# Convolution taps in PSUM banks, the norm's multiply on GpSimd, and output sums in tiles of their own: a convolution and SwiGLU layer on one core

## The chip, the cores and the metric

The kernel runs on one core of a Trainium2 chip, as one launch. The metric is the device time in microseconds (us), the median of several runs. A core has TensorE (PE, matrix products, with its weight loads shown as PEld), VectorE (DVE), ScalarE (ACT) and GpSimd (POOL); SyncE (SP) issues the DMA transfers. SBUF is the working memory, PSUM the eight banks of 128 x 512 fp32 that TensorE writes.

## The reference

```python
def _attn_ref(x, weight):              # x (8, 4096, 192), weight (8 heads, 7 taps)
    w = np.exp(weight - np.max(weight, axis=-1, keepdims=True))
    w = w / (np.sum(w, axis=-1, keepdims=True) + 1e-09)
    x_pad = np.concatenate([np.zeros((B, K - 1, D)), x], axis=1)
    idx = np.arange(S)[:, None] + np.arange(K)[None, :]
    x_unf = x_pad[:, idx, :].reshape(B, S, K, H, D // H)
    return np.einsum('hk,bskhg->bshg', w, x_unf).reshape(B, S, D)

def _moe_ref(x, w_gate, w_val, w_out, rms_g):   # x (32768, 192), d_ff 1536
    rms = np.sqrt(np.mean(x * x, axis=-1, keepdims=True) + 1e-06)
    xn = x / rms * rms_g
    g = xn @ w_gate
    silu = g * (1.0 / (1.0 + np.exp(-g)))
    val = xn @ w_val
    return (silu * val @ w_out).astype(np.float32)
```

A causal convolution of seven taps, whose weights each head has of its own, feeds a layer with an RMS norm, two projections from 192 to 1536, silu(g) * val, and a projection back to 192. All is in fp32.

## The kernel before

**Tiling.** The 32768 tokens are cut into 32 "pairs", each two tiles of T = 512 tokens (g = 0 and 1). The 1536 hidden features are twelve chunks of 128; three chunks and both token tiles make a "unit", four units to a pair. The value h = silu(g) * val of a unit lies in a tile `ht` of six slices of 128 x 512, v = 0 to 2 for g = 0 and 3 to 5 for g = 1.

**The product stage** of a pair. Both projections are done with 15 products a unit where 18 would be plain: sums of the inputs (`XSUM`, line 67, made by `x_sum` into `xc`, eleven a pair) and of the weights go in, and the results are combined afterwards. TensorE's rows are used in halves: the half LOW makes gate results (h = 0), UPP value results (h = 1). A matmul of 64 x 512 is one step; a pair has 4 x 15 x 2 = 120 such steps (`product`, line 693, recorded at L699). Each half has four PSUM banks, taken from and given back to the lists `free`.

`Unit.do` (line 705) holds the small operations between the banks. Their names in the order are engine (A, V, G, D for ScalarE, VectorE, GpSimd, DMA), action, half or step, and unit:

- S40, S50, S41, ...: copy a bank to a temporary tile of 128 x 512 (L660 on ScalarE, L664 on VectorE). F0, F2, F3: copy one bank to another.
- D5: add a temporary to a bank (L715). C: the sum "c" of the temporaries 40 and 50 (L719). R0 to R5: a bank plus or minus a temporary (L725), into a temporary for the gate and into `ht` for the value.
- G: silu on ScalarE (L738). M: multiply silu by value into `ht` (L745); M4 reads the value from a bank, the others from `ht`.

The temporaries come from the list `tiles`, first in, first out: 5 single ones, 6 in two `tls` tiles, and 3 in the tile `nt`, 14 in all.

**The output stage** of a pair. The projection back is again made with fewer products: seven "forms" of six steps k where eight would be plain, 126 steps in all (`OUTS`, line 764, `products`, line 803, recorded at L817). The left sides are h itself and four sums of h (`sum`, line 838, recorded at L845, 24 a pair on GpSimd): form 1 of `sum` overwrites a21, form 2 a11, form 4 a12, and form 3 goes to the tile `early`. Three banks (X, Y, Z) collect the results; VectorE adds them (L863) and transposes blocks into `o_sb` (L833), which is stored.

**Work for later pairs**, in the same streams: x of pair p + 3 is loaded (`load`); pair p + 2 gets its convolution, seven operations "cv" of 128 x 1536 (`tap`, L413 on ScalarE for the first, L417 on VectorE for the rest), the squares "sq" on ScalarE (L429), their reduction "red" on VectorE (L440 to L442), the power -1/2 "pow" on GpSimd (L446, L449), the spreading of the factors "bc" (two copies at L454 and a transpose at L458) and the multiply "mul" (L465), all on VectorE; the result goes to DRAM ("place") and comes back transposed as `xb` of pair p + 1 ("fetch", L613), from which the x sums "X" are made (L622).

**The order** of all this is written out by hand, in `ORDER` (line 90), one list for every pair: "p2" is two TensorE steps, "VR1.0.0" result 1 of half 0 of unit 0 on VectorE; a name that ends in "-" acts for the pair before. Every engine runs its own instructions in this order and waits by semaphores for what it needs. Pair 0 has a start of its own (`START`, `LATER`, `plain`, `outer`).

Of the kernel before, what the change touches and what calls it, by code (L numbers as in the profile page):

```python
# [11 lines left out]
F32 = mybir.dt.float32  # L12
# [7 lines left out]
def kernel(  # L20
# [67 lines left out]

    SPAN = 1509
    ORDER = (  # L90
        "p2 Dplace- VT12- p2 AS40.0.0 AS40.1.0 p2 VF0.0.0 AF0.1.0 p2 VT22- AS50.1.0 Dst0-",
        "VS50.0.0 p2 AS41.0.0 VS41.1.0 Acv0 GC.0.0 p2 VS00.1.0 Dst1- p2 GC.1.0 VD5.1.0",
        "AS00.0.0 p2 VD5.0.0 AS42.1.0 AS42.0.0 p2 AS51.0.0 VR1.0.0 AS51.1.0 p2 VR1.1.0",
        "AG1.0.0 VR0.0.0 p2 AF2.0.0 VR0.1.0 AF2.1.0 p1 AF3.0.0 VF3.1.0 p2 AS44.0.0 p1",
        "AS44.1.0 VR5.0.0 p2 VR2.0.0 AG5.0.0 p1 VR2.1.0 AG2.0.0 p2 VR3.1.0 AG4.0.0 GM2.1.0 p1",
        "VR5.1.0 p1 AS40.0.1 VR3.0.0 p1 AS40.1.1 p1 VM4.1.0 AF0.0.1 p1 AG3.0.0 p1 VF0.1.1",
        "AS50.0.1 p1 Vcv1 p1 AS50.1.1 GC.0.1 p1 AS41.0.1 p1 AS41.1.1 p1 GC.1.1 AS00.0.1 p1",
        "AS00.1.1 VD5.0.1 p2 GM5.1.0 VD5.1.1 AS42.0.1 p1 AS42.1.1 p1 VR1.0.1 AS51.1.1 p1",
        "GM1.1.0 AS51.0.1 p1 VR1.1.1 p1 VR0.0.1 p1 AF2.0.1 VR0.1.1 p1 AF2.1.1 p1 Vcv2 AF3.0.1",
        "p1 AF3.1.1 p1 AS44.0.1 p1 AS44.1.1 p1 VR5.0.1 AG1.0.1 p1 VR2.1.1 p1 AG0.0.0 p1",  # L100
        "VR2.0.1 GM0.1.0 p1 AG4.0.1 VR3.1.1 p2 VM4.1.1 AS40.0.2 GM3.1.0 p1 VR3.0.1 AS40.1.2",
        "p1 AG5.0.1 VR5.1.1 p1 GM1.1.1 AF0.0.2 p1 VS50.0.2 AF0.1.2 p2 AS50.1.2 GS3.0 VS41.0.2",
        "p1 AG2.0.1 p1 AS41.1.2 VS00.0.2 p1 GS3.1 AG0.0.1 p1 VC.1.2 AS00.1.2 p2 GS1.0 VD5.1.2",
        "AS42.0.2 p1 AS42.1.2 VD5.0.2 p1 GC.0.2 VR1.0.2 p1 AS51.0.2 p1 AS51.1.2 VR1.1.2 p1",
        "GM2.1.1 VR0.0.2 p1 AF2.0.2 p1 VR0.1.2 AF2.1.2 p1 AG3.0.1 p1 AF3.0.2 p1 GM3.1.1",
        "VS44.0.2 AF3.1.2 p1 AS44.1.2 p1 VR2.0.2 AG1.0.2 p2 VR2.1.2 AG0.0.2 p1 VR5.0.2",
        "AG2.0.2 GM0.1.2 p1 VR5.1.2 AG4.0.2 p2 VR3.1.2 AS40.0.3 GM5.1.1 p1 AG5.0.2 VR3.0.2 p1",
        "AS40.1.3 VM4.1.2 p1 GM1.1.2 AF0.0.3 p1 VS50.0.3 AF0.1.3 p2 VM0.1.1 AS50.1.3 GS1.1 p1",
        "AS41.0.3 VS41.1.3 p1 AS00.0.3 p1 VM5.1.2 GS3.2 AG3.0.2 p1 VD5.0.3 AS00.1.3 p2",
        "VD5.1.3 AS42.0.3 GS1.2 p1 AS42.1.3 VS51.0.3 p1 AS51.1.3 VR1.0.3 p1 GM2.1.2 p2",  # L110
        "VR0.1.3 p1 GC.0.3 AF2.0.3 p1 VR1.1.3 AF2.1.3 p1 VR0.0.3 GM3.1.2 p1 VF3.1.3 p1",
        "AF3.0.3 p1 AS44.0.3 VC.1.3 GS3.4 p1 AS44.1.3 VR2.0.3 p1 AG1.0.3 p1 VR5.0.3 AG0.0.3",
        "GS3.3 p1 VR5.1.3 AG4.0.3 VR3.0.3 p2 AG5.0.3 GS1.3 p1 VM0.1.3 p1 AG2.0.3 p1 VM1.1.3",
        "p2 AG3.0.3 p1 GS2.1 Dfetch VR2.1.3 p3 Vcv3 p2 GS2.0 p6 Ac1 VM4.1.3 p3 Vcv4 p1 GS3.5",
        "p6 GS2.3 p2 VM5.1.3 p3 VR3.1.3 p1 GS1.5 p2 As7 p1 VX3 p2 GS2.2 p1 VM3.1.3 p3 VM2.1.3",
        "p2 GS1.4 Vcv5 p6 GS2.4 p3 VX0 p3 GS2.5 Vcv6 p6 GS4.5 p2 VX1 p1 Asq p2 VX2 GS4.0 p3",
        "VT11 p1 Ac2 p1 Dload p1 GS4.2 Vred p6 GS4.4 p4 VX4 p1 Gpow p1 VX7 p3 VX8 p3 VX9 p3",
        "VX6 p1 GS4.1 p4 VC22 p2 VX5 GS4.3 p3 Vbc p3 Vmul p12 VC21 p2 VX10 p3 VT21",
    )

    cst = ctx.enter_context(tc.tile_pool(name="cst", bufs=1))
# [100 lines left out]
    kept = [early[:, i].rearrange("p (j d) -> p j d", d=D) for i in range(3)]  # L222
    kept = itertools.cycle(kept)
    flat3 = early[:].rearrange("p i n -> p (i n)")
    diff = [flat3[:, k * T : (k + 1) * T] for k in range(FC // 2)]
    nw = 4 * (FC // 2) * (D // 2)
    tw = x0[:].rearrange("p j d -> p (j d)")[:, 0:nw].rearrange(
        "p (i k d) -> p i k d", i=4, k=FC // 2
# [178 lines left out]
    def tap(p, k, eng="V"):  # L407
# [12 lines left out]
        if k == K - 1:  # L420
            x_sb.pop(p)

    yn, st = {}, {}
    nb = TB // Q

# [18 lines left out]
    def factor(p):  # L444
# [2 lines left out]
            out=r, in0=r, scalar1=1.0 / D, scalar2=1e-6, op0=ALU.mult, op1=ALU.add  # L447
        )
        nc.gpsimd.tensor_tensor(out=r, in0=r, in1=nhalf[:, 0 : nb * NR], op=ALU.pow)  # L449

    def spread(p):
        ss, t, r = st[p]
        for c in range(nb):
            nc.vector.tensor_copy(  # L454
                out=by_head(t)[:, c],
                in_=r[:, c, :].rearrange("p (b o) -> p b o", o=1).to_broadcast([P, NR, H]),
            )
        nc.vector.transpose(out=ss[:], in_=t[:])  # L458

    def scale(p):  # L460
        ss = st.pop(p)[0]
        y = y_of(p)
        ys.pop(p)
        yn[p] = yn[p][:].rearrange("p (a t) -> p a t", t=TB)
        nc.vector.tensor_tensor(  # L465
            out=yn[p].rearrange("p a t -> p t a"), in0=y,
            in1=ss[:].rearrange("p (t o) -> p t o", o=1).to_broadcast([P, TB, GS]), op=ALU.mult,
        )
# [177 lines left out]
    def put(at, do):  # L646
        heapq.heappush(line, (at, next(tick), do))
# [25 lines left out]
    class Unit:  # L673
# [31 lines left out]
        def do(self, eng, act, h):  # L705
# [9 lines left out]
                nc.vector.tensor_tensor(out=b, in0=b, in1=t[:], op=ALU.add)  # L715
                tiles.append(t)
            elif kind == "C":
                c, t = tl.pop(("40", h)), tl.pop(("50", h))
                engine[eng].tensor_tensor(out=c[:], in0=c[:], in1=t[:], op=ALU.add)  # L719
                tl["c", h] = c  # L720
                tiles.append(t)
            elif kind == "R":
                k, s = RESULT[v]
                t = tl.pop((k, h))
# [31 lines left out]
    def out_sums():  # L756
# [5 lines left out]
                yield  # L762

    OUTS = (
        (1, "X", 0, 6), (7, "Z", 0, 6), (2, "Y", 0, 6), (6, "X", 0, 6), (4, "Z", 0, 3),
        (5, "X", 0, 6), (4, "Z", 3, 6), (3, "X", 0, 6),
    )
    HOME = {"X": 0, "Y": 1, "Z": 1}
    RIGHT = {1: B11, 2: B21, 3: B22, 4: T4, 5: T1, 6: T2, 7: T3}

    class Pair:
# [9 lines left out]
        def left(self, form, k):  # L781
            if form == 7:
                return diff[k]
            g, f = {1: (0, 0), 6: (0, 0), 2: (0, 1), 3: (0, 1), 5: (1, 0), 4: (1, 1)}[form]
            return self.h(g, 2 * k + f)

        def bank(self, b):
# [50 lines left out]
        def sum(self, form, k, eng):  # L838
            a11, a12 = self.h(0, 2 * k), self.h(0, 2 * k + 1)
            a21, a22 = self.h(1, 2 * k), self.h(1, 2 * k + 1)  # L840
            dst, a, b, op = {
                1: (a21, a21, a22, ALU.add), 2: (a11, a21, a11, ALU.subtract),
                3: (diff[k], a11, a21, ALU.subtract), 4: (a12, a12, a11, ALU.subtract),
            }[form]
            engine[eng].tensor_tensor(out=dst, in0=a, in1=b, op=op)  # L845

# [36 lines left out]
        def ahead(self, eng, act):  # L883
# [4 lines left out]
            elif act == "load":  # L888
                load(p + 3)
            elif p + 2 < PAIRS:  # L890
                if act[0:2] == "cv":
                    tap(p + 2, int(act[2:]), eng)
                else:
                    {
                        "sq": square, "red": reduce, "pow": factor, "bc": spread, "mul": scale,
                        "place": lambda p: done(place(p)),
                    }[act](p + 2)
# [185 lines left out]
    base = NU * SPAN  # L1083
    put(base - 1, lambda: outer(0, hts, base))
    put(base + 450, functools.partial(fetch, 1))
    put(base + 1317, lambda: tiles.extend(t[:, i, :] for t in tl6 for i in range(3)))
    put(base + 3000, lambda: tiles.extend(flat[:, i * T : (i + 1) * T] for i in range(3)))
    c = base + 200

    def later(it, *places):  # L1090
# [58 lines left out]
```

## Time and profile before

| | before |
|---|---|
| time, median of 3 runs | 3021.5 us (3017.94 to 3021.96) |
| span of the profiled run | 3016.8 us |
| VectorE busy | 2802.2 us (93%) |
| TensorE busy | 2741.1 us (91%) |
| GpSimd busy | 2226.0 us (74%) |
| ScalarE busy | 1648.5 us (55%) |
| chain that ended last: PE, DVE, issue | 55%, 32%, 8% of the span |
| DVE taps of 1536 (L417), 186 | 427.0 us |
| DVE multiply of the norm (L465), 31 | 90.1 us |
| GpSimd sums of h (L845), 744 | 996.0 + 290.6 us |

Busy times are summed over the whole span and are averages over stages that differ. The chain of waits is followed back from the last instruction to what released each; its shares say which engine the end waited for. A row of a group gives the line of the kernel, engine, operation, outputs and inputs with shapes, the count, then busy time in us and the mean of one in ns, then the idle time before it and what ended that.

### The profile page before, as it was taken

To read this page: it belongs to the slowest core of one execution; us is meant where nothing else is said; L and a number is where in the kernel's file an instruction comes from. 1 tells how busy PE (TensorE), PEld (TensorE's weight loads), DVE (VectorE), ACT (ScalarE), POOL (GpSimd) and SP (SyncE) were. 2 spreads that over 40 slices of the span, in tenths; PEclk is the share of its full clock that TensorE was granted. 3 is DMA by queue.
4 is the path that set the end of the run, shared out by engine and by line. 5 is a ranking of instruction groups with operands and counts; after the bars stand their busy time and mean duration, and the time that the engine had idled before them with its cause. 6 is when DMAs were issued, how large, how long until landed. Compare 5 with 4: busy or idle time off the path is not lost.

```text
span 3016.8 us, 91662 instructions
## 1 busy us (share of the span) xinstructions
PE 2741.1 (91%) x39418; PEld 1883.3 (62%) x39418; DVE 2802.2 (93%) x3655; ACT 1648.5 (55%) x3061; POOL 2226.0 (74%) x1513
## 2 busy tenths in 40 slices
PE   6999988999889998889988899988999889999999
PEld 3665666655666566666666665666666666666666
DVE  8899999999999999999999999999999999999986
ACT  5366544566445664446654466544566445665455
POOL 4886678866778767787667886677866778766777
PEclk9999999999999999999999999999999999999999
DMA  5412122121222112221222212122111222122110
GB/s 125 76 26 51 34 56 55 31 47 34 55 56 34 43 34 55 55 39 38 48 41 56 44 40 49 34 55 55 34 43 34 55 55 35 43 42 47 44 34 13
DMA packets 445208, 139.33 MB, mean 46 GB/s; under 512 B 385024, under 2 KB 419328, under 8 KB 444673
## 3 DMA queue, kind: packets, MB, share of 16 engines
q1 hardware_dynamic: 444240, 133.44, 22.3%
q8 instruction: 308, 5.05, 0.7%
q14 instruction: 100, 0.82, 0.1%
q10 hardware_dynamic: 560, 0.03, 0.0%
HBM read 83.87 MB, written 49.55 MB: 44 GB/s over the span
## 4 chain that ended last, share of the span: by engine, by line
PE 55%; DVE 32%; issue 8%; POOL 2%; DMA 1%; ACT 1%; SPq 1%; DVEq 0%; ACTq 0%; POOLq 0%
PE ps L699 52%; DVE xc L622 9%; DVE ht L745 8%; DVE y L417 6%; PE ps L817 2%; DVE o_sb L833 2%; DVE s L440 2%; DVE s L454 1%; DVE ht L725 1%; POOL ht L845 1%; PE ps L913 1%; POOL wf L346 1%; ACT tls L738 1%; DVE nt L863 0%; DVE tile L863 0%
## 5 line engine op out<-in xcount | busy, mean ns | idle before, releaser
L699 PE MATMUL ps<-xc,wf 64*128 64x512 f32 x4960 | 1344.8, 600 | 33.0 <-DVE o_sb L833 19.5
L699 PEld LDWEIGHTS ps<-xc,wf 64*128 64x128 f32 x4960 | 665.5, 187 | 555.9 <-issue 331.7
L845 POOL TENSOR_TENSOR ht<-ht 128x512 f32<-128x512 f32 x558 | 996.0, 1806 | 9.7
L699 PE MATMUL ps<-xb,wf 64*128 64x512 f32 x2480 | 751.3, 595 | 0.0
L817 PE MATMUL ps<-ht,wo_sb 128*32 128x128 f32 x13392 | 419.5, 280 | 69.5 <-DVE nt L863 27.1
L660 ACT ACTIVATE tile<-ps 128x512 f32<-128x512 f32 (+1 forms) x508 | 297.1, 599 | 330.4 <-PE ps L699 316.3
L699 PEld LDWEIGHTS ps<-xb,wf 64*128 64x128 f32 x2480 | 340.3, 188 | 216.1 <-issue 181.0
L660 ACT ACTIVATE tls<-ps 128x512 f32<-128x512 f32 x678 | 389.1, 602 | 123.3 <-PE ps L817 69.8
L817 PEld LDWEIGHTS ps<-ht,wo_sb 128*32 128x32 f32 x13392 | 381.4, 113 | 118.1 <-POOL r L449 46.9
L660 ACT ACTIVATE ps<-ps 128x512 f32<-128x512 f32 (+1 forms) x651 | 349.2, 579 | 190.7 <-PE ps L817 87.6
L817 PE MATMUL ps<-ht,x 128*32 128x128 f32 x13392 | 392.3, 274 | 54.1 <-POOL ht L845 37.8
L417 DVE SCALAR_TENSOR_TENSOR y<-xh,tp,y 128x1536 f32<-128x1536 f32 x186 | 427.0, 2296 | 0.2
L817 PEld LDWEIGHTS ps<-ht,x 128*32 128x32 f32 x13392 | 365.9, 110 | 75.4 <-POOL ht L845 51.7
L745 POOL TENSOR_TENSOR ht<-ht,tile 128x512 f32<-128x512 f32 x195 | 251.2, 1299 | 214.3 <-ACT tile L738 214.3
L660 ACT ACTIVATE nt<-ps 128x512 f32<-128x512 f32 (+1 forms) x302 | 175.0, 594 | 304.1 <-PE ps L817 157.3
L745 POOL TENSOR_TENSOR ht<-ht,tls 128x512 f32<-128x512 f32 x145 | 194.0, 1338 | 147.5 <-ACT tls L738 147.5
L845 POOL TENSOR_TENSOR early<-ht 128x512 f32<-128x512 f32 x186 | 290.6, 1578 | 0.0
L817 PE MATMUL ps<-early,x 128*32 128x128 f32 x4464 | 154.0, 287 | 84.7 <-issue 56.0
L719 POOL TENSOR_TENSOR tile<-tile,tls 128x512 f32<-128x512 f32 x51 | 86.9, 1711 | 180.4 <-DVE tls L664 134.5
L429 ACT ACTIVATE yn<-y 128x1536 f32<-128x1536 f32 x31 | 46.0, 1485 | 296.5 <-DVE y L417 296.5
L817 PEld LDWEIGHTS ps<-early,x 128*32 128x32 f32 x4464 | 133.9, 115 | 97.2 <-issue 63.0
L725 DVE TENSOR_TENSOR ht<-ps,tls 128x512 f32<-128x512 f32 x287 | 193.3, 679 | 0.2
(140 smaller groups left out, 3578.7 us busy)
## 6 DMA issues: line engine op xcount, KB each, us to landing
xb<-xd SPq DMA_DIRECT2D x124, 384.0 KB
out_dram<-o_sb SPq DMA_DIRECT2D x64, 384.0 KB
xd<-yn SPq DMA_DIRECT2D x248, 96.0 KB
xh<-in_x_dram SPq DMA_DIRECT2D x192, 105.0 KB
xh<-in_x_dram SPq DMA_DIRECT2D x56, 98.4 KB
ht<-in_moe_w_gate_dram SPq DMA_DIRECT2D x12, 192.0 KB
ht<-in_moe_w_val_dram SPq DMA_DIRECT2D x12, 192.0 KB
tls<-in_moe_w_out_dram SPq DMA_DIRECT2D x8, 192.0 KB
```

Source lines behind the costliest of these rows:

```text
L417: nc.vector.scalar_tensor_tensor(out=y, in0=xk, scalar=w, in1=y, op0=ALU.mult, op1=ALU.add)
L429: nc.scalar.activation(out=yn[p][:].rearrange("p (t a) -> p t a", a=GS), in_=y_of(p), func=AF.Square)
L440: nc.vector.tensor_reduce(out=ss[:], in_=sq, axis=AX.X, op=ALU.add)
L622: e.tensor_tensor(out=xc[:, d, :], in0=x_op(a), in1=x_op(b), op=ALU.add)
L660: nc.scalar.activation(out=dst, in_=src, func=AF.Copy, scale=float(s))
L699: nc.tensor.matmul(out=self.new(v, h, True) if first else self.old(v, h), lhsT=wf[self.u][HALF[h], WAT[i], :], rhs=x_op(XOP[i])[HALF[h]], ...
L719: engine[eng].tensor_tensor(out=c[:], in0=c[:], in1=t[:], op=ALU.add)
L725: nc.vector.tensor_tensor(out=self.hv(v) if h else t[:], in0=self.old(v, h), in1=t[:], op=plus(s))
L745: engine[eng].tensor_tensor(out=self.hv(v), in0=src, in1=t[:], op=ALU.mult)
L817: nc.tensor.matmul(out=self.bank(b)[q * Q : (q + 1) * Q, m * P : (m + 1) * P], lhsT=RIGHT[form][:, k, m, :], rhs=cols[:, q], start=(first ...
L833: nc.vector.transpose(out=to[:, m, n], in_=src[:, m * P : (m + 1) * P].rearrange("p (b e) -> p b e", e=Q),)
L845: engine[eng].tensor_tensor(out=dst, in0=a, in1=b, op=op)
```

## The change

The change moves work off VectorE, takes VectorE operations with two SBUF inputs away, and orders everything anew.

1. The convolution (`part_tap`) is cut into three parts of 512 columns. Its first tap is written by ScalarE into a PSUM bank, five more are accumulated there by VectorE, and the last goes from the bank to `y` in SBUF. Each VectorE tap so has one input in SBUF and one in PSUM. The parts take banks of half 0, 1 and 0 (`SIDE`).
2. The norm: the two spreading copies and the multiply of 128 x 1536 go from VectorE to GpSimd, also in the start.
3. The sum "c" takes the bank 5 itself, not a copy of it: all eight are on VectorE, and the eight copies S50 are gone. Of the multiplies M0, M1, M2, M3 and M5, GpSimd makes 18 a pair where it made 13, VectorE 2 where it made 7; GpSimd makes four of the eleven x sums (X0, X1, X4, X7), which VectorE made.
4. The sums of h no longer overwrite what other forms read: the sum for form 6 goes to six slices `both`, and that for form 3 for k > 1 to four slices `rest`. These slices come from `early`, `nt`, a new tile `more` and the two `tls`. Nine temporaries are left in `tiles`. Form 2 is cut in two, and its second half comes last.
5. `ORDER` is a new list, with the same 120 + 126 TensorE steps.

```diff
+    NK = FC // 2
+    held = [flat3[:, k * T : (k + 1) * T] for k in range(9)]
+    more = work.tile([P, 2, T], F32, name="more")
+    diff, both, rest = held[0:NK], held[NK:], [more[:, i] for i in range(2)]
...
+    def part_tap(p, k, j):
+        cut = slice(j * T, (j + 1) * T)
+        xf = x_sb[p][:].rearrange("p t a -> p (t a)")
+        xk, w = xf[:, k * GS + j * T : k * GS + (j + 1) * T], tp[:, k : k + 1]
+        if k == 0:
+            h = SIDE[j]
+            acc[p, j] = h, pick(h, False)
+            nc.scalar.mul(bank(*acc[p, j])[:], xk, w)
+            return
+        at = bank(*acc[p, j])[:]
+        dst = at
+        if k == K - 1:
...
+            dst = ys[p][:].rearrange("p j d -> p (j d)")[:, cut]
+        nc.vector.scalar_tensor_tensor(
+            out=dst, in0=xk, scalar=w, in1=at, op0=ALU.mult, op1=ALU.add
+        )
...
-    def spread(p):
-        ss, t, r = st[p]
+        t, r = st[p][1:]
         for c in range(nb):
-            nc.vector.tensor_copy(
+            nc.gpsimd.tensor_copy(
...
-    def scale(p):
+    def scale(p, eng="G"):
...
-        nc.vector.tensor_tensor(
+        e = nc.gpsimd if eng == "G" else nc.vector
+        e.tensor_tensor(
             out=yn[p].rearrange("p a t -> p t a"), in0=y,
...
             elif kind == "C":
-                c, t = tl.pop(("40", h)), tl.pop(("50", h))
-                engine[eng].tensor_tensor(out=c[:], in0=c[:], in1=t[:], op=ALU.add)
-                tl["c", h] = c
-                tiles.append(t)
+                t = tl["c", h] = tl.pop(("40", h))
+                nc.vector.tensor_tensor(out=t[:], in0=self.old(5, h), in1=t[:], op=ALU.add)
...
     OUTS = (
-        (1, "X", 0, 6), (7, "Z", 0, 6), (2, "Y", 0, 6), (6, "X", 0, 6), (4, "Z", 0, 3),
-        (5, "X", 0, 6), (4, "Z", 3, 6), (3, "X", 0, 6),
+        (1, "X", 0, 6), (7, "Z", 0, 6), (2, "Y", 0, 3), (6, "X", 0, 6), (4, "Z", 0, 3),
+        (5, "X", 0, 6), (4, "Z", 3, 6), (3, "X", 0, 6), (2, "Y", 3, 6),
     )
+    SIDE = (0, 1, 0)
...
             dst, a, b, op = {
-                1: (a21, a21, a22, ALU.add), 2: (a11, a21, a11, ALU.subtract),
-                3: (diff[k], a11, a21, ALU.subtract), 4: (a12, a12, a11, ALU.subtract),
+                1: (a21, a21, a22, ALU.add), 2: (both[k], a21, a11, ALU.subtract),
+                3: (diff[k], a11, a21, ALU.subtract),
+                4: (rest[k - 2] if k > 1 else a12, a12, both[k], ALU.subtract),
             }[form]
...
-    put(base + 1317, lambda: tiles.extend(t[:, i, :] for t in tl6 for i in range(3)))
-    put(base + 3000, lambda: tiles.extend(flat[:, i * T : (i + 1) * T] for i in range(3)))
+    both.extend(flat[:, i * T : (i + 1) * T] for i in range(NK - len(both)))
+    rest.extend(t[:, 2, :] for t in tl6)
+    put(base + 1317, lambda: tiles.extend(t[:, i, :] for t in tl6 for i in range(2)))
```

The end of the new `ORDER`, from the last products of a pair to the end of its output stage, with the multiply and the last x sum in the first rows of the next pair:

```diff
+        "p2 VT22- AS40.1.0 VT11- p2 AS40.0.0 Dload- Vbc- p2 AF0.0.0 VC.0.0 Dst1- AF0.1.0",
+        "Dst0- p2 Gmul- p2 AS41.1.0 VC.1.0 AS41.0.0 p2 AS00.1.0 VS00.0.0 p2 GX7- VD5.0.0 p2",
...
+        "AG0.0.3 VR5.0.3 p3 GM1.1.3 VR3.0.3 GS3.4 VR2.0.3 p1 GS4.3 Acv0_2 p1 VR3.1.3 p1",
+        "Vcv1_2 p2 AG4.0.3 p1 AG3.0.3 p1 GM3.1.3 p1 Dfetch VM4.1.3 Acv0_1 p3 Acv0_0 p2",
+        "AG2.0.3 p2 Vcv1_0 p1 VR5.1.3 p1 GS1.4 VR2.1.3 p1 Vcv1_1 p1 GS3.5 p1 Ac1 p1 AG5.0.3",
+        "p4 Vcv2_2 p2 GS2.4 p6 Vcv2_0 p1 VM5.1.3 p3 Vcv2_1 As7 p2 Vcv3_2 p1 Vcv3_0 p1 GS1.5",
+        "p4 Vcv3_1 p1 GS4.1 p1 Vcv4_0 p2 Vcv5_0 GS2.5 p3 GS4.0 Vcv4_2 p5 Vcv4_1 p1 Vcv5_2 p3",
+        "GX0 Vcv5_1 p5 VX3 Ac2 Vcv6_2 p3 VX2 p7 VX8 p4 GM2.1.3 Vcv6_0 VX6 VM0.1.3 p9 Vcv6_1",
+        "p1 Asq p2 GX1 GS4.5 p3 VC22 p2 GS4.4 p2 Vred p6 VC21 p2 VX5 p4 VX10 p3 VX9 VT21 p2",
+        "Gpow p4 VT12 p3 GX4 p3",
```

## The prediction

> **What bounds the kernel now.** I read the busy shares first, then the same busy times by stage, then the chain of waits through one pair, and last the durations of single operations.
>
> ```profile
> PE 2741.1 (91%) x39418; PEld 1883.3 (62%) x39418; DVE 2802.2 (93%) x3655; ACT 1648.5 (55%) x3061; POOL 2226.0 (74%) x1513
> ```
>
> VectorE and TensorE are both above 90%, so the average names no bound. The stages do. The fetch of the next pair's x is issued once a pair, at the end of its products; these issues stand at 198.24 us (pair 1) and 2895.05 us (pair 30), so a period is 2696.8 / 29 = 92.99 us. I cut one period, and the two last pairs, where products end and begin:
>
> ```profile
> core 0: us, PE busy (x) PEld busy (x) DVE busy (x) ACT busy (x) POOL busy (x), PEclk, DMA share, GB/s
> 1543.10:1594.60 51.50, 51.50 (x236) 29.31 (x236) 46.78 (x71) 45.22 (x86) 34.53 (x26) 1.00 0.11 29
> 1594.60:1635.80 41.20, 32.25 (x1016) 27.65 (x1014) 40.96 (x43) 6.18 (x10) 34.79 (x20) 1.00 0.38 66
> ...
> 2895.10:2928.80 33.70, 30.35 (x1011) 28.92 (x1010) 28.11 (x29) 3.61 (x7) 27.99 (x18) 0.95 0.22 51
> ...
> 2981.50:3011.00 29.50, 28.42 (x1009) 27.14 (x1008) 12.84 (x19) 3.33 (x7) 23.66 (x18) 1.00 0.02 4
> ```
>
> The product stage takes 51.5 us and TensorE is busy in all of it. The output stage takes 41.2 us and there VectorE is busy for 40.96, TensorE for 32.25. The two last rows are a natural experiment. Pair 30 has no convolution or norm to do for a later pair, and its output stage took 33.7 us at a mean clock of 0.95; pair 31, which prepares nothing at all, took 29.5. So the output stage owes some 12 us to what VectorE does for later pairs. The chain of waits agrees: some 51 us of products, then VectorE operation after operation (start and length in us):
>
> ```profile
> 1599.40 2.16 DVE y L417
> ...
> 1602.08 2.22 DVE y L417
> 1604.30 1.68 DVE ht L745
> 1605.98 0.60 DVE ht L725
> ...
> 1613.78 1.69 DVE xc L622
> ...
> 1634.50 1.21 DVE o_sb L833 x6
> ```
>
> The single durations say why VectorE needs that long:
>
> ```profile
> L417 DVE SCALAR_TENSOR_TENSOR y<-xh,tp,y 128x1536 f32<-128x1536 f32 x186 | 427.0, 2296 | 0.2
> L725 DVE TENSOR_TENSOR ht<-ps,tls 128x512 f32<-128x512 f32 x287 | 193.3, 679 | 0.2
> L465 DVE TENSOR_TENSOR yn<-y,s 128x1536 f32<-128x1536 f32 x31 | 90.1, 2907 | 1.1
> L845 POOL TENSOR_TENSOR ht<-ht x558: 1267/1722/2800, 178.0 to 3004.1; 128x512 f32<-128x512 f32 x186
> L417 DVE SCALAR_TENSOR_TENSOR y<-xh,tp,y x186: 1807/2230/2836, 50.9 to 2822.4; 128x1536 f32<-128x1536 f32 x186
> L745 DVE TENSOR_TENSOR ht<-ht,tls x94: 865/1750/1806, 188.5 to 2989.9; 128x512 f32<-128x512 f32 x94
> L622 DVE TENSOR_TENSOR xc<-xb,xc x155: 647/685/1782, 126.2 to 2919.2; 128x512 f32<-128x512 f32 x155
> ```
>
> The three numbers with strokes are minimum, median and maximum in ns. An operation with one input in PSUM (L725) is 0.68 us every time. One of the same size with both inputs in SBUF is 0.65 at best and 1.75 to 1.8 beside GpSimd; GpSimd's sum (L845) is 1.27 alone, 1.72 in the median, 2.80 at worst. 1.27 + 0.5 is 1.77: the two take turns.
>
> [...]
>
> **The change part by part**, per pair.
>
> (1) Taps. Six VectorE taps of 1536 elements (L417), 6 x 2.30 = 13.8 us, become 18 of 512 with one PSUM input. No row is this exact form; the nearest (L725) is 0.68, and 0.60 apart where two follow each other in the chain. 18 x 0.62 = 11.2 us, at most 18 x 0.69 = 12.4 if a tap must wait for the one before it on its bank. First tap: ScalarE, three of about 0.58 for one of 1.57; ScalarE is busy for 6.2 of 41.2 us of the output stage. Three banks are held, 2 and 1 by half, all closed before the next products.
>
> (2) Norm. The multiply (2.91) and the two spreading copies (2 x 0.69) leave VectorE: -4.3 us. GpSimd gains a multiply of 1536 elements with a strided output: 3 x 1.27 = 3.8 at least, 3 x 1.75 = 5.3 beside contention, 6 if the stride costs; I take 4.5. The copies: 0.25 (its smallest copies now, 0.24 and 0.26) to 0.69 each. The multiply runs at the start of the next products. Behind it is queued only the sum X7, whose reader is the 12th product of the first unit, at 23 of 120 steps = 9.9 us in. Multiply from about 2 to 6.5, X7 to 8: in time, with 2 us to spare. New waits: the transpose of the norm factors on VectorE now waits for GpSimd's copies, which by the order end some 1 us into the products; behind it on VectorE is the first sum "c", which the order asks for only at 2.6 us. The write of yn to DRAM waits for the multiply, and is read back only at the end of that period.
>
> (3) Fewer two-SBUF operations. Value multiplies on VectorE go from 7 (1.51 each, L745) to 2, x sums from 11 (1.08) to 7: -7.6 and -4.3 us. (VectorE's x sum X5 now waits for GpSimd's X1; the order puts 15 steps of 0.24 us, 3.6 us, between them, and X1 alone takes 1.3.) The 8 sums "c" (6 GpSimd, 2 VectorE) become 8 VectorE operations with the bank as input: +8 x 0.68 - 2 x 1.17 = +3.1, and 8 copies "50" go, 5 of them ScalarE's; other copies move to VectorE, together +3 x 0.69 = +2.1. Two-SBUF operations of VectorE in all: 27 before, 9 after.
>
> (4) h sums in own tiles: the sum for form 6 no longer overwrites the input of form 1, nor the sum for form 3 (mostly) that of form 2, so a GpSimd sum need not wait for TensorE and the second half of form 2 can come last; today GpSimd waits for TensorE nowhere in the table of waits, so I give this nothing. The price is temporaries: 9 tiles for 14. Nearest reuse by the order: a ScalarE copy 2 steps (0.9 us) after the VectorE operation that frees its tile, and two VectorE copies 5 steps (2.2 us) after a GpSimd multiply. In the product stage these are queued before products, so a late GpSimd would stop TensorE there.
>
> **Sums.** VectorE: -13.8 + 11.2 - 4.3 - 7.6 - 4.3 + 3.1 + 2.1 = -13.6 us of a 92.7 us period. In the output stage by the new order: 5 results and a multiply from PSUM 6 x 0.60 = 3.6, taps 11.2, norm reductions 2.2, two output sums 1.0, two groups of transposes 1.3, and 9 two-SBUF operations: 5.9 at 0.66, 15.8 at 1.75, 10.6 at the present means. Together 25.2 / 29.9 / 35.1. In the product stage 46.8 less two taps (1.8 and 2.0), two multiplies (0.9 and 1.2) and a result (0.6), plus the 3.1 and 2.1 of part 3 is 45.6 of 51.5 us: hidden under the products, as now.
>
> GpSimd: 24 h sums at 1.27 (30.5), 18 multiplies (22.9), 4 x sums (5.1), pow 2.5, copies 0.7, multiply 4.5 = 66.2, plus 9 x 0.5 for turns with VectorE = 70.7; at most 24 x 1.73 + 18 x 1.30 + 7 + 2.5 + 1.4 + 6 = 81.8. Today, by its rows, 69.6. At 70.7 it is hidden in a period of 83 us. In the output stage it has 17 such operations and the pow, 25 us.
>
> TensorE: 1008 records at 120 in 3.48 us = 29.2 us. So the output stage goes from 41.2 to the longer of 29.2 (TensorE) and 29.9 (VectorE), plus joints: I add 1.6 us for one pause such as TensorE makes before single groups of these matmuls now (1.90 us at 1510.27, 2.83 us at 2906.73), giving 31.5. Products 51.5; the mean period is 92.99 - 92.7 = 0.3 longer than one at full clock. Period 83.3 us.
>
> **The rivals.**
> A (the forecast): the output stage ends with TensorE and VectorE about level. 198.2 + 29 x 83.3 + 121.8 = 2736, and 4 us between span and time: 2740. The head and tail I leave alone: the multiply on GpSimd may add 2 us before pair 1, the last pairs may gain as much.
> B: VectorE still bounds the output stage, each of the 9 operations waiting a full GpSimd one: 35.1. For it: GpSimd is busy 34.8 of 41.2 us there now. Against it: by the new order GpSimd has 25 us of work in 30, so an operation often meets it idle or half done. 29 x 86.9 + 324 = 2844.
> C: GpSimd becomes the bound at 81.8 us and its lag delays output sums and the multiply: some 89 us a period, 2905. Against it: its long durations come from 27 VectorE operations of which 9 remain.
> D: the 9 tiles. If once in each of four units TensorE waits 3 us for a tile from GpSimd, and the output stage gets only to 35: 51.5 + 12 + 35 = 98.5 or more, 3180: slower. Against it: GpSimd needs 41 us in 51.5 there, and now waits 362 us in all for ScalarE's silu results (214.3 and 147.5 in the table of waits): it is ahead.
>
> **How the numbers follow.** A 0.66, B 0.20, C 0.08, D 0.06. A alone, with the output stage from 29.3 (no joint) to 33, spans 2676 to 2783; the range reaches to B, 2680 to 2850, and leaves out C, D and the outer edges of A and B, some 2 in 10. Only D is slower; 0.01 falls at no change.
>
> **What would show it.** Right: output stages of about 31 us with TensorE busy over 90%; taps at 0.6 to 0.7; GpSimd's h sums with a median near 1.3; no multiply of 1536 on VectorE. Wrong: a tap above 0.8; VectorE busy through a stage of 35 (B); TensorE waiting for GpSimd's sums (C), or for ScalarE copies in the product stage (D); a GpSimd multiply above 6 us.

## The result and the profile after

The changed kernel takes 2791.22 us (2789.73 to 2805.57, four runs) where the kernel before takes 3019.72 us in the same session: a ratio of 0.9254, with a 95% interval of 0.9222 to 0.9285. The span of the profiled run went from 3016.8 to 2787.9 us, 228.9 us less. The first lines are the busy shares and the chain of waits, from the page of the changed kernel.

```profile
PE 2650.6 (95%) x39418; PEld 1826.5 (66%) x39418; DVE 2400.9 (86%) x3914; ACT 1505.7 (54%) x2778; POOL 2078.4 (75%) x1695
...
PE 77%; DVE 9%; issue 6%; POOL 3%; ACT 2%; DMA 1%; SPq 1%; POOLq 0%; DVEq 0%
```

VectorE lost 401 us of work (2802.2 to 2400.9) and its share of the chain fell from 32% to 9%; TensorE's rose from 55% to 77%. The bound has moved to TensorE. The stages show how far. The rows below are windows of the changed kernel (length, busy time and count of PE, PEld, DVE, ACT and POOL, granted clock, DMA share, GB/s): the products of one pair, its output stage, the output stage of the next pair, and that of the last.

```profile
core 0: us, PE busy (x) PEld busy (x) DVE busy (x) ACT busy (x) POOL busy (x), PEclk, DMA share, GB/s
1422.33:1474.88 52.55, 52.55 (x240) 28.35 (x240) 46.45 (x80) 40.18 (x76) 41.55 (x33) 1.00 0.16 37
1474.88:1506.12 31.24, 29.04 (x1009) 27.25 (x1008) 28.92 (x46) 6.76 (x11) 23.43 (x20) 1.00 0.42 74
1558.68:1594.17 35.49, 30.92 (x1010) 29.78 (x1009) 27.54 (x44) 6.76 (x11) 22.39 (x20) 0.90 0.35 64
2754.50:2783.50 29.00, 28.42 (x1009) 27.34 (x1008) 8.51 (x18) 3.25 (x7) 16.48 (x13) 1.00 0.02 5
```

TensorE is busy for every microsecond of the products. In the output stages VectorE is no longer busy to the end (28.92 of 31.24, 27.54 of 35.49), and yet they are longer than TensorE's 29.04 and 30.92: something stops TensorE that isn't VectorE. I cut all 31 ordered pairs at TensorE's first product and first output matmul; these are the means in us, for all kernels told of here.

| kernel | products | output stage | time, us |
|---|---|---|---|
| before | 55.57 | 37.00 | 3019.72 |
| after | 52.61 | 32.62 | 2791.22 |
| e1, no fetch of x | 52.60 | 28.94 | 2675.57 |
| e2, fetch twice | 52.62 | 35.84 | 2889.13 |
| e3, fetch spread, SyncE | 52.61 | 30.79 | 2729.40 |
| e9, half of it from ScalarE's queue | 52.61 | 29.80 | 2698.43 |
| e12, all of it from ScalarE's queue | 52.61 | 29.53 | 2695.53 |
| e4, before with the fetch spread | 55.68 | 36.91 | 3020.16 |
| e6, taps in SBUF again | 52.61 | 37.97 | 2954.25 |
| e7, norm's multiply on VectorE | 54.78 | 32.86 | 2872.48 |
| e13, the same, later | 55.74 | 32.51 | 2883.85 |
| e8, two-SBUF operations back | 53.75 | 32.51 | 2820.30 |
| e10, form 6 in place | 52.61 | 33.19 | 2809.15 |
| e11, before with parts 1 and 2 | 52.83 | 37.96 | 2971.73 |

Before and after differ by 2.96 us in the products and 4.37 in the output stage; 31 x 7.33 = 227 us is nearly the whole difference of 228.9. The 2.96 us are mostly the joint: before, TensorE began the products and at once waited, until 1.6 and 3.4 us in, for VectorE to finish the last output stage's sums (L863) and transposes (L833). In the timeline of the kernel before, for a pair that began at 1632.39:

```profile
1633.96 1.12 PE L699 MATMUL ps<-xc,wf 64*128 64x512 f32 x2 [0.45 <-DVE tile L863]
1635.76 1.25 PE L699 MATMUL ps<-xc,wf 64*128 64x512 f32 x4 [0.67 <-DVE o_sb L833]
```

By the starts of its matmuls, 2.7 of the 2.96 us are lost in these first steps. After, they aren't.

The single operations answer to the rows of before; these are groups of the changed kernel (busy us, mean ns, idle time before and what ended it).

```profile
L445 DVE SCALAR_TENSOR_TENSOR ps<-xh,tp,ps 128x512 f32<-128x512 f32 x435 | 299.8, 750 | 16.7 <-ACT ps L437 15.6
L882 POOL TENSOR_TENSOR early<-ht 128x512 f32<-128x512 f32 x279 | 354.7, 1276 | 9.7
L882 POOL TENSOR_TENSOR ht<-ht 128x512 f32<-128x512 f32 x186 | 238.2, 1281 | 30.1 <-DVE ht L776 20.4
L498 POOL TENSOR_TENSOR yn<-y,s 128x1536 f32<-128x1536 f32 x31 | 89.9, 2900 | 26.9 <-issue 26.9
```

A tap of 512 columns with one input in PSUM takes 750 ns. GpSimd's h sums into `early` take 1276 ns in the mean where it was 1578, and those from `ht` into `ht` 1281 where it was 1806: nearly all turns with VectorE are gone (all 744 sums have a median of 1.28 us, and a mean of 1.31). The multiply takes 2.90 us on GpSimd, as it did on VectorE (2907 ns).

What stops TensorE stands in the timeline of the changed kernel, in the longer of the two output stages (start, length, count; in brackets the idle time before the row and what ended it):

```profile
1558.68 4.14 PE L853 MATMUL ps<-ht,wo_sb 128*32 128x128 f32 x144
1562.64 2.79 PE L853 MATMUL ps<-early,x 128*32 128x128 f32 x93
1569.43 2.98 PE L853 MATMUL ps<-early,x 128*32 128x128 f32 x50 [4.00 <-issue]
```

For 4.00 us TensorE does nothing in the middle of a run of like matmuls, and no semaphore ends the wait: "issue" is time in which the engine waited for nothing that the profile shows. The data was there: GpSimd's last sum into these tiles is this row of the same timeline, and it ends at 1564.35, before the pause begins at 1565.43.

```profile
1563.05 1.30 POOL L882 TENSOR_TENSOR early<-ht 128x512 f32<-128x512 f32 x1
```

What else runs then is in the transfers of the changed kernel between 1560 and 1570 us (packets, MB, share of 16 engines):

```profile
DMA packets 812, 1.55 MB, mean 155 GB/s; under 512 B 64, under 2 KB 64, under 8 KB 811
...
q1 hardware_dynamic: 811, 1.53, 68.0%
q8 instruction: 1, 0.02, 0.9%
```

The fetch of the next pair's x (1.5 MB in four transfers) has most of the DMA engines' time, and one packet of instructions in queue q8 gets through. In the next 10 us, when the fetch is over, it is three:

```profile
q8 instruction: 3, 0.05, 2.2%
```

In the whole run q8 carried 308 packets with 5.05 MB, 16 KB each. TensorE's 39418 matmuls and as many weight loads are 78836 instructions, 256 to a packet; and the chain shows the output matmuls in runs of 127 and 128, 3.70 us each, which with as many weight loads are 256 again. So the reading, an estimate from these counts, is that q8 brings TensorE's instructions, and that TensorE, which here uses up a packet of them every 3.7 us, ran dry behind the fetch.

The trace (the file behind these views) has the time of every packet, and bears this out. The packet beside the pause above ran from 1566.57 to 1567.94, and TensorE went on 1.49 us after it. Each of the 55 pauses over 0.3 us in the output stages of the changed kernel ends 1.20 to 1.75 us after a packet of q8 has landed; of the output matmuls at large, one in nine starts so long after one. In the waits of the changed kernel (us, times, longest) this is the row:

```profile
PE ps L853 <- issue: 96.4, 61, 4.2
```

### The profile page after: what moved, and what is told of

It reads as the page before. It is cut to its first block, busy times and chain, and to the rows that moved or that the text cites. A ratio compares the mean times of both kernels' runs of the same rounds, so it can differ in the third digit from the quotient of the medians.

```text
span 2787.9 us, 91977 instructions
## 1 busy us (share of the span) xinstructions
PE 2650.6 (95%) x39418; PEld 1826.5 (66%) x39418; DVE 2400.9 (86%) x3914; ACT 1505.7 (54%) x2778; POOL 2078.4 (75%) x1695
## 3 DMA queue, kind: packets, MB, share of 16 engines
q8 instruction: 308, 5.05, 0.8%
## 4 chain that ended last, share of the span: by engine, by line
PE 77%; DVE 9%; issue 6%; POOL 3%; ACT 2%; DMA 1%; SPq 1%; POOLq 0%; DVEq 0%
PE ps L732 56%; PE ps L853 19%; DVE xc L655 3%; DVE ps L445 1%; POOL ht L882 1%; PE ps L990 1%; DVE ht L756 1%; ACT ps L437 1%; PE ps L950 1%; DMA xh<-in_x_dram 1%; POOL nt L882 1%; DVE y L445 1%; DVE s L471 1%; DVE o_sb L869 1%; POOL xc L655 1%
## 5 line engine op out<-in xcount | busy, mean ns | idle before, releaser
L776 POOL TENSOR_TENSOR ht<-ht,tile 128x512 f32<-128x512 f32 x330 | 418.7, 1276 | 196.0 <-ACT tile L769 177.2
L693 ACT ACTIVATE tls<-ps 128x512 f32<-128x512 f32 (+1 forms) x513 | 293.0, 588 | 437.5 <-PE ps L853 253.1
L776 POOL TENSOR_TENSOR ht<-ht,tls 128x512 f32<-128x512 f32 x228 | 290.5, 1277 | 113.9 <-ACT tls L769 103.5
L882 POOL TENSOR_TENSOR early<-ht 128x512 f32<-128x512 f32 x279 | 354.7, 1276 | 9.7
L445 DVE SCALAR_TENSOR_TENSOR ps<-xh,tp,ps 128x512 f32<-128x512 f32 x435 | 299.8, 750 | 16.7 <-ACT ps L437 15.6
L756 DVE TENSOR_TENSOR tile<-ps,tile 128x512 f32<-128x512 f32 x371 | 250.8, 684 | 25.3 <-ACT tile L693 21.8
L882 POOL TENSOR_TENSOR ht<-ht 128x512 f32<-128x512 f32 x186 | 238.2, 1281 | 30.1 <-DVE ht L776 20.4
L853 PE MATMUL ps<-ht,x 128*32 128x128 f32 x8928 | 258.7, 273 | 1.6 <-issue 1.0
L853 PEld LDWEIGHTS ps<-ht,x 128*32 128x32 f32 x8928 | 247.1, 110 | 8.1 <-issue 7.8
L769 ACT ACTIVATE tile<-tile 128x512 f32<-128x512 f32 x371 | 230.3, 628 | 0.0
L756 DVE TENSOR_TENSOR ht<-ps,tile 128x512 f32<-128x512 f32 x333 | 222.9, 684 | 4.6
```

What stands on the lines that cost most here:

```text
L445: nc.vector.scalar_tensor_tensor(out=dst, in0=xk, scalar=w, in1=at, op0=ALU.mult, op1=ALU.add)
L693: nc.scalar.activation(out=dst, in_=src, func=AF.Copy, scale=float(s))
L756: nc.vector.tensor_tensor(out=self.hv(v) if h else t[:], in0=self.old(v, h), in1=t[:], op=plus(s))
L769: nc.scalar.activation(out=t[:], in_=src[:], func=AF.Silu)
L776: engine[eng].tensor_tensor(out=self.hv(v), in0=src, in1=t[:], op=ALU.mult)
L853: nc.tensor.matmul(out=self.bank(b)[q * Q : (q + 1) * Q, m * P : (m + 1) * P], lhsT=RIGHT[form][:, k, m, :], rhs=cols[:, q], start=(first ...
```

## The experiments

The theories at this point: N, the pauses are instructions held behind the fetch; G, they are late sums of GpSimd; T, the gain is that VectorE's operations no longer take turns with GpSimd; V, VectorE's total still sets the period; S, the order counts and not where the inputs lie. Times of before in these sessions are 3021.9 to 3022.6 us, some 2.5 us above those beside the changed kernel, so a difference of a few us between a run and the changed kernel is no finding.

**e1: no fetch.** From pair 2 on `xb` keeps what it had.

```diff
-                    fetch(p + 1) if act == "fetch" else x_sum(int(act[1:]), eng)
+                    None if act == "fetch" else x_sum(int(act[1:]), eng)
```

> The changed kernel with the fetch of xb left out for all pairs after pair 1 (the x sums and products then work on the old xb, so the output differs; every instruction of the engines stays). Theory N (TensorE's pause early in the output stage is its instruction stream, which waits behind the 1.5 MB fetch in the DMA engines): the pause of 1 to 4 us is gone, output stage 29.5 to 30.5 us instead of 32.8, period about 82.5 instead of 85.3, time 2700 to 2720 us. Rival G (the pause is TensorE waiting for GpSimd's sums in the tile early, the left side of form 7): the pause stays, 2780 to 2800 us.

2675.57 us, ratio 0.8851 (0.8834 to 0.8869). One output stage, from the windows of this run, and TensorE's row in its waits:

```profile
1255.22:1284.08 28.86, 28.30 (x1009) 27.52 (x1009) 27.11 (x44) 6.74 (x11) 22.89 (x20) 1.00 0.19 25
```

```profile
PE ps L853 <- issue: 7.6, 17, 0.9
```

VectorE's and GpSimd's work is about the same as in the changed kernel, 27.11 and 22.89 us, but the stage is 28.86 us long with TensorE busy for 28.30. The pauses are nearly gone (96.4 to 7.6 us), and with them 3.68 us of each output stage, more than N expected (2700 to 2720 us). So the fetch is their cause, and 28.94 us is what the stage takes without it.

**e2: the fetch twice.** The same 1.5 MB are fetched again at the same place; the new argument only keeps the source for the second time.

```diff
-                    fetch(p + 1) if act == "fetch" else x_sum(int(act[1:]), eng)
+                    (fetch(p + 1, True), fetch(p + 1)) if act == "fetch" else x_sum(int(act[1:]), eng)
```

> The changed kernel with every fetch of xb made twice, one after the other. Theory N: the pause grows by about the time of another fetch, 6 us, to 8 or 9 us a pair; time about 2791 + 30 x 6 = 2960 us, at least 2900. Rival G: the pause stays at 1 to 4 us; only the x sums start 6 us later, which have some 10 us of room, time 2790 to 2830 us.

2889.13 us, ratio 0.9558 (0.9539 to 0.9577). The waits of this run:

```profile
PE ps L853 <- issue: 171.5, 94, 5.0
```

The pauses grow with the traffic, 96.4 to 171.5 us, and the output stage by 3.22 us, half of what N expected, so that the time just misses its 2900 us: the pauses become more in number (61 to 94), the longest only from 4.2 to 5.0 us. In the trace, the second four transfers are issued from 3.8 to 12.0 us into the output stage, 1.65 us apart or more, and not on top of the first, which fits. All 92 pauses over 0.3 us here end 1.25 to 1.72 us after a packet of q8 too. The mean granted clock of the run is 0.979, against 0.989 after and 0.997 in e1, so a pause may cost more than its own length. In the changed kernel, the 15 output stages without a pause over 2.6 us ran at 1.00; of the 15 with one, 11 ran at 0.90 to 0.95.

**e3 and e4: the fetch spread over the products,** in the changed kernel and in the kernel before. Its four transfers stand at steps 110, 113, 128 and 138 of the pair, where all four were at 128; in the trace SyncE issues those as the products end.

```diff
-        "Vcv1_2 p2 AG4.0.3 p1 AG3.0.3 p1 GM3.1.3 p1 Dfetch VM4.1.3 Acv0_1 p3 Acv0_0 p2",
...
-    def fetch(p):
+    def fetch(p, some=(1, 0), halves=(0, 1)):
...
-                    fetch(p + 1) if act == "fetch" else x_sum(int(act[1:]), eng)
+                    fetch(p + 1, [int(act[1])], [int(act[2])]) if act[0] == "f" else x_sum(int(act[1:]), eng)
```

> The changed kernel with the fetch cut into its four transfers and spread: the two of g = 0 at steps 110 and 113, still in the products, the two of g = 1 at steps 128 and 138. Theory N: no transfer holds TensorE's instructions for more than some 2 us[...]; the pause goes to under 0.5 us, output stage about 30, time 2705 to 2735 us. Rival G: nothing changes, 2780 to 2800 us.

> The kernel before with the same spreading of the fetch. Both theories of the pause agree with the prediction's first step, that VectorE bounds the output stage there: the pause (1 to 4 us in the profile of before too) vanishes by theory N, but the time stays, 3000 to 3025 us, the x sums being at most a little earlier. If TensorE's pause counted there too, 29 x 2.5 us would come off, about 2950 us.

e3: 2729.40 us, ratio 0.9032 (0.9019 to 0.9046). e4: 3020.16 us, ratio 0.9992 (0.9984 to 1.0001), no change. The same edit is worth 62 us in one kernel and nothing in the other. In the kernel before, TensorE paused just so, but under VectorE's work. These are a group and a wait of before, and the same group of e4, which shows where the time goes when the pause is taken away.

```profile
L817 PE MATMUL ps<-early,x 128*32 128x128 f32 x4464 | 154.0, 287 | 84.7 <-issue 56.0
PE ps L817 <- POOL early L845: 28.7, 17, 3.6
L816 PE MATMUL ps<-early,x 128*32 128x128 f32 x4464 | 142.0, 275 | 65.6 <-POOL early L844 50.1 <-issue 15.4
```

The wait for "issue" was 56.0 us before and is 15.4 here, while the wait for GpSimd's sums on the same matmuls went from 28.7 to 50.1. e3 still has pauses of 52.5 us, and the queue of SyncE shows why:

```profile
1355.44 6.51 SPq L645 DMA_DIRECT2D xb<-xd  x4
```

The four issues lie within 6.51 us. Two go out some 5.6 us before the products end and two as they end; within each two SyncE waits for nothing, and they are 0.6 to 0.7 us apart, so that step 138 comes with step 128. Their place in the order alone doesn't hold them apart. (That instructions held for some 2 us make no pause over 0.5 us was an estimate of theory N; no run shows it.)

**e9 and e12: transfers from ScalarE's queue.** ScalarE comes by its place in the order, since it waits for banks on the way: in e9, where the last two transfers are its own (steps 128 and 141), they go out some 4.1 us apart. In e12 all four are its own (steps 109, 114, 131 and 151): two go out some 5.6 and 4.3 us before the output stage, one around 1 us into it or sooner, and one 4.2 us or more into it.

```diff
+    def fetch(p, some=(1, 0), halves=(0, 1), q=nc.sync):
...
-                nc.sync.dma_start(
+                q.dma_start(
```

> As e3_fetch_early, but the two transfers of g = 1 are issued by ScalarE's queue, at steps 128 and 141, where ScalarE waits for TensorE's work in order; in e3 SyncE issued both at once when the products ended, and 52 us of pauses were left. Theory N: at most one quarter of the fetch (1.6 us) stands before TensorE's instructions at a time; output stage 29.5 to 30.2 us, time 2690 to 2715 us. Rival: it is the bytes and not their bunching, or the store and load of x that hold the instructions: 2725 to 2735 us as in e3.

> As e9_fetch_scalar, with all four transfers in ScalarE's queue, further apart: steps 109, 114, 131 and 151. Theory N: the pauses left in e9 (0.9 us a pair) shrink, 2680 to 2698 us; the kernel with no fetch, 2675.6, is the floor. Rival: the last transfer lands too late for the x sums, and TensorE waits at the start of the products: over 2705 us.

e9: 2698.43 us, ratio 0.8931 (0.8918 to 0.8944). e12: 2695.53 us, ratio 0.8920 (0.8907 to 0.8933). A window and TensorE's wait, both of e12:

```profile
933.50:963.35 29.85, 28.64 (x1009) 27.40 (x1008) 27.59 (x46) 6.74 (x11) 23.43 (x20) 1.00 0.33 55
```

```profile
PE ps L852 <- issue: 27.6, 47, 1.9
```

The whole fetch is there and the pauses are down to 27.6 us: what hurts is the burst, not the bytes. (From e3 to e9 the queue changes together with the spacing; no run has the one without the other.) e12 is the best version found, 96 us below the changed kernel and 20 above the one without a fetch; the two intervals overlap, so e9 and e12 aren't told apart.

**e6: the taps accumulate in `y` in SBUF,** in the same three parts and the same order.

```diff
-            nc.scalar.mul(bank(*acc[p, j])[:], xk, w)
-            return
-        at = bank(*acc[p, j])[:]
...
+            nc.scalar.mul(ys[p][:].rearrange("p j d -> p (j d)")[:, cut], xk, w)
+            return
+        at = dst = ys[p][:].rearrange("p j d -> p (j d)")[:, cut]
```

> The changed kernel with the three parts of the taps accumulated in y in SBUF instead of in PSUM banks; order, cutting and engines stay. Theory T (what the change gains is that VectorE's operations no longer take turns with GpSimd): a tap of 512 goes from 0.75 us to between 1.0 and 1.75, 18 of them add 6 to 18 us to an output stage in which VectorE is busy 28 of 32.7 us; stage 37 to 45, time 2900 to 3150 us. Rival S (the gain is the new order and the move out of the product stage, wherever the sums lie): taps stay at 0.7 to 0.8, 2780 to 2810 us.

2954.25 us, ratio 0.9775 (0.9755 to 0.9795), 163 us above the changed kernel. The taps in the groups of this run, and a window of it:

```profile
L442 DVE SCALAR_TENSOR_TENSOR y<-xh,tp,y 128x512 f32<-128x512 f32 x522 | 658.8, 1305 | 1.0
```

```profile
1013.76:1052.90 39.14, 31.82 (x1010) 29.95 (x1009) 36.65 (x46) 5.96 (x10) 26.91 (x20) 0.91 0.39 65
```

With the same shape, count and place, a tap takes 1305 ns in the mean for 750 because its accumulator is in SBUF. SBUF isn't slower in itself: in the trace, the 134 taps of e6 beside which GpSimd ran no operation with two inputs took 736 to 753 ns, and the 388 beside one 1500 in the mean, while the 376 such taps of the changed kernel took 757 at most. So the difference is the turns with GpSimd. It is 18 x 0.555 = 10 us more of VectorE a pair, and the output stage is 5.35 us longer. This is the largest of the parts tried.

**e7 and e13: the norm's multiply on VectorE again,** at its place (e7) or at step 59 in the middle of the products (e13, with the write to DRAM at step 66).

```diff
-        "Dst0- p2 Gmul- p2 AS41.1.0 ...
+        "Dst0- p2 Vmul- p2 AS41.1.0 ...
```

> The changed kernel with the norm's multiply of 1536 back on VectorE, at the same place in the order, at the start of the next products. Theory T: VectorE is busy 46.5 of 52.6 us in the product stage, so 1.7 to 2.9 us more there is nearly hidden; TensorE may wait up to 1 us a pair for banks: 2790 to 2825 us. Rival V (VectorE's total still sets the period): the whole 2.9 us is paid, 29 x 2.9 = 84 us, about 2875.

> As e7_mul_dve (the multiply of 1536 on VectorE), which cost 81 us, but 51 steps later, in the middle of the products (step 59), with the write to DRAM after it. Theory Q (it is the place: at the start of the products VectorE's queue still holds the transposes that give TensorE its banks, and runs late): in the middle the 2.8 us are mostly hidden, 2795 to 2825 us. Rival R (the product stage has no room for an operation of 2.8 us anywhere, since the banks wait for every VectorE operation within a few steps): about 2870 us, as in e7.

e7: 2872.48 us (four runs, 2862.63 to 2884.16), ratio 0.9514 (0.9481 to 0.9548), 81 us above the changed kernel, and my theory of 2790 to 2825 fell. It costs in the products (52.61 to 54.78), hardly in the output stage (32.62 to 32.86): once a pair, TensorE waits 1.5 us there for the sum "c" (L752), which is queued behind the multiply and goes to a slice of `tls` or a single tile. The first of the two in the waits of e7:

```profile
PE ps L732 <- DVE tls L752: 22.7, 15, 1.5
```

I took this for a question of the place; e13 says no: 2883.85 us, ratio 0.9538 (0.9522 to 0.9554), with the products at 55.74; the two are not told apart. In the timeline of e13:

```profile
1050.52 2.95 DVE L497 TENSOR_TENSOR yn<-y,s 128x1536 f32<-128x1536 f32 x1
1053.33 0.67 DVE L755 TENSOR_TENSOR ht<-ps,tile 128x512 f32<-128x512 f32 x1
1054.05 1.89 PE L731 MATMUL ps<-xc,wf 64*128 64x512 f32 x5 [1.59 <-DVE ht L755]
```

The result that frees a bank stands behind the multiply, and TensorE waits 1.59 us for the bank. In the waits of e13 this is 29 times, once a pair:

```profile
PE ps L731 <- DVE ht L755: 46.6, 29, 1.6
```

By the starts of TensorE's matmuls, all of the 3.1 us that e13 loses in the products is lost here: 2.15 by the late start after the wait and the rest within the next six steps. VectorE is busy for 46.45 of 52.55 us of the products in the changed kernel, but by the order it frees a bank every step or two, and neither place tried has room for one operation of 2.9 us. V's number for e7 (2875) came out, but not its cause: VectorE is idle there for 5.8 us of the products and 5.3 of the output stage, and the loss stands at one place.

**e8: nine two-SBUF operations back on VectorE** (X0, X1, X4, X7 and five multiplies).

```diff
-        "GX0 Vcv5_1 p5 VX3 Ac2 Vcv6_2 p3 VX2 p7 VX8 p4 GM2.1.3 Vcv6_0 VX6 VM0.1.3 p9 Vcv6_1",
+        "VX0 Vcv5_1 p5 VX3 Ac2 Vcv6_2 p3 VX2 p7 VX8 p4 VM2.1.3 Vcv6_0 VX6 VM0.1.3 p9 Vcv6_1",
```

> The changed kernel with the four x sums and five of the value multiplies back on VectorE, in the same places (18 two-SBUF operations of VectorE a pair instead of 9). Theory T: seven of the nine stand in or at the edge of the output stage, at 1.1 to 1.75 us each 8 to 12 us more for VectorE, which has 4 to 5 us idle there: stage 36 to 40, time 2880 to 3010 us. Rival S: they cost 0.66 each, 4.6 us in all, which the idle time takes: 2790 to 2815 us.

2820.30 us, ratio 0.9332 (0.9313 to 0.9350): 29 us above the changed kernel, between both theories. Turns are rarer than before: an x sum takes 0.92 us and a multiply 0.93 where I had 1.08 and 1.51 from before. And the output stage has slack for VectorE (32.51, where it was 32.62); what is lost is 1.1 us in the products.

**e10: form 6 in place again.** The six sums overwrite a11, at steps where TensorE has read it. The sums that output form 3 takes for k = 2 and 3 here read a11 before, not after, the sum for form 6.

```diff
-                1: (a21, a21, a22, ALU.add), 2: (both[k], a21, a11, ALU.subtract),
+                1: (a21, a21, a22, ALU.add), 2: (a11, a21, a11, ALU.subtract),
```

> The changed kernel with the six sums for form 6 again in place of form 1's input, and so all six ordered after form 1's steps (133 to 169), where the change has four of them in the product stage. Theory H (the own tiles let GpSimd make sums in the product stage, where it has room): 4 x 1.28 = 5.1 us more for GpSimd in an output stage where it is busy 23 of 32.7 us, with waits for TensorE's form 1 in front of it; TensorE waits 1 to 4 us a pair for form 6: 2820 to 2910 us. Rival P (as predicted: the own tiles are worth nothing): 2780 to 2800 us.

2809.15 us, ratio 0.9299 (0.9283 to 0.9314), between both theories: the tiles of their own are worth some 18 us, little above the noise, since this interval touches that of the changed kernel (up to 0.9285); the output stage is 0.57 us longer. With its own tiles, four of the six sums can run during the products; in place, they come late, and TensorE waits in all 8.6 us for GpSimd's sums into `early` and 6.4 for those into `ht`.

**e11: parts 1 and 2 alone,** put into the kernel before and its order, with two results moved forward so that their banks are free for the taps.

> The kernel before with parts 1 and 2 alone: taps in three PSUM banks, all in the output stage, spreading and multiply on GpSimd, at the steps the changed kernel has them; two results moved forward to free their banks. Theory T: VectorE's output stage is 41 us less 9.9 (four old taps), 2.8 (multiply), 1.3 (spreading) plus 18 x 0.68 = 12.2, that is 39, or 36 if the other two-SBUF operations meet GpSimd less: 2870 to 2960 us, less than half of the gain. Rival I (taps and norm are the change, the rest is tidying): 2780 to 2830 us.

2971.73 us, ratio 0.9827 (0.9813 to 0.9842): 51 of the 228 us, less than either theory gave. A window of e11:

```profile
1015.52:1054.87 39.35, 32.28 (x1009) 30.28 (x1008) 34.50 (x49) 6.57 (x11) 27.71 (x22) 0.91 0.39 65
```

The joint is gone, the products are at 52.83; but the output stage is 0.96 us longer than before, with VectorE at 34.5 us of 39.35 and TensorE at a granted clock of 0.91; TensorE waits 127 us in all for VectorE's output sums (L894). Undone one at a time, the parts cost 163 (taps), 81 (multiply), 29 (two-SBUF operations) and 18 us (tiles), 291 together; done first, the two largest gain 51. The parts aren't additive. That each counts only once the others have brought VectorE below TensorE fits this, but no run shows it part by part. What the new order is worth by itself, the cut of form 2 and the slices `rest` weren't tried.

## Why the prediction was right, and where it wasn't

**The likeliest case.** The bound moved from VectorE to TensorE, as A had it; of the rivals, B is false (VectorE is busy for only 27.5 of 35.49 us of an output stage), C is false (GpSimd is busy for 41.55 + 23.43 = 65 us of a period of 85.3), D is false (TensorE waits for nothing in the products, 52.55 of 52.55). The period between fetches is 85.32 us where 83.3 was forecast, and 2791 lies 51 us above 2740, inside the range. The number alone would not tell A from B: it is about as far from B's 2844, and 8 us above what A alone spanned, so that it is inside only because the range reached to B. The stages tell them apart: the output stage, 32.62 us, lies within A's 29.3 to 33.

**The term that was mis-sized is "1.6 us for one pause".** I had seen the pauses (1.90 and 2.83 us), and the page had 56.0 us of "issue" on these matmuls, but I charged them as a constant and didn't ask what caused them. By e1 against after they are 3.68 us a pair, 2.08 more than I put in. The fetch is issued at the end of the products, so its transfers run in the first part of the output stage, and since VectorE there is no longer the slower of the two, nothing hides it. The natural experiment of the prediction held the hint: pair 31 with its 29.5 us is also the pair that fetches nothing.

**The other terms of the period.** TensorE's and VectorE's common 29.9 is 28.94 (-0.96). The products are 52.61, not 51.5 (+1.11): my cut put the first of them into the output stage of 41.2, which also held the joint of 2.96. There is no further 0.3 for the mean. Together 2.08 - 0.96 + 1.11 - 0.3 = 1.9 of the 2.0 us by which the period is longer; 29 such periods are 59 us, and the 51 missing are these, less some 7 us that the head and tail gained. That the errors are of both signs and partly cancel is luck.

**Part 1.** Taps at 0.62 a piece, at most 0.69: 0.75 each (the longest of 522 took 0.757, below the 0.8 that was a sign of being wrong), though ten of them in a row took 6.80 us, 0.68 apart. The term is 18 x 0.06 = 1.1 us too small and did no harm, since VectorE has slack. That the taps leave the turns with GpSimd is what e6 shows: 1.305 us with the accumulator in SBUF, 1.500 beside GpSimd's operations with two inputs, against 0.75 with it in PSUM, the plainest case of it here.

**Part 2.** The multiply on GpSimd was 2.90 us, not 4.5 (3.8 to 6; that a strided output costs up to 6 was a guess, from no row): that is 1.9 ns an element, where the sums I scaled from take 2.5 ns. The multiply reads a tile and a broadcast factor and is three times as long, the sums read two tiles; no run tells whether the second input or a fixed cost of each operation makes the difference. It was in time, as forecast. That the multiply on VectorE would cost 81 us in the new order I had not seen: in the sum it is a part of the 4.3 us that leave VectorE; its cost lies in what would stand behind it, in the products (e7, e13), not in the total.

**Part 3.** GpSimd's sums fell to 1.28 us in the median, as "what would show it" had it, and products of 45.6 of 51.5 us for VectorE were 46.45 of 52.55. But nine of its operations put back cost only 29 us (e8), none of it in the output stage, where VectorE has room by now.

**Part 4.** "I give this nothing" was 18 us too little (e10), in the output stage. "GpSimd waits for TensorE nowhere" no longer holds after the change; these are two rows of the waits of the changed kernel (us, times, longest):

```profile
POOL ht L882 <- PE ps L853: 132.0, 31, 7.7
...
DVE xc L655 <- POOL xc L655: 93.2, 30, 10.1
```

The sums for form 3 with k = 0 and 1 overwrite a12, which form 2 reads first, and GpSimd now reaches them before TensorE has. The x sum X0 is queued behind them on GpSimd, and a VectorE x sum waits for that. It can cost little, since TensorE waits for VectorE's last transposes (L869) only 4.9 us in all; it is a new wait that I hadn't named.

## What to carry to other kernels

When the bound of a stage is lifted, the stage gains only down to the next thing beneath it. Look for that thing by the pauses and not by busy shares: the "issue" pauses of TensorE beside a burst of DMA are read, by the times of the packets of q8, as instructions that came late (all 55 over 0.3 us ended 1.20 to 1.75 us after a packet). Spread a bulk transfer: half of it moved from the output stage (1009 matmuls in 31.24 us) into the products (240 in 52.55) saved 62 us (e3), though that the fewer instructions are the reason no run shows by itself. And issue it from an engine that reaches its place in the order only when that time has come: from ScalarE's queue, two transfers saved 31 us more and all four 34 (e9, e12). An operation moved to another engine is worth what stands behind it in its old queue: the multiply of 2.9 us cost TensorE 2.2 and 3.1 us a pair (e7, e13), three quarters of its length or more, though VectorE was idle for 6 of the 52.55 us of the products in the changed kernel.

## What the runs showed of the hardware that was not expected

TensorE stood still beside data transfers for which the profile shows no wait of it: beside a fetch of 1.5 MB it paused for up to 4.2 us, in all 96.4 us of the changed kernel; removing the fetch saved 116 us and spreading it 96. That the fetch causes the pauses is shown by e1, e2, e3, e9 and e12 (7.6 us of them without the fetch, 171.5 with it twice, 52.5 and 27.6 with it spread in e3 and e12). That it does so through the instruction stream (q8, with 0.9% of the DMA engines' time beside 68.0% for the data, between 1560 and 1570 us) is read from the packets: each of the 55 longer pauses ends 1.20 to 1.75 us after one has landed, and the profile shows no other releaser; no run holds the instructions back by anything but data. A long pause goes with a lower granted clock, and so may cost more than its length: the output stage with 4.00 us of pause ran at 0.90, with TensorE busy for 30.92 us where it was 29.04 at 1.00, and the mean clock was 0.997 without the fetch, 0.989 with it and 0.979 with it twice.
